# Asking for two chunks' inputs at once, moving a recurrence into the first part, and grouping attention products by kind

## Chip, cores and metric

One core of one Trainium2 chip. The metric is the device time of one launch in microseconds (us). Each kernel is run several times; nearly all times below are medians.

## The reference, cut to what matters

```python
# batch 4, heads 8, sequence 768, head dim 64
for t in range(S):
    state = gamma * state + outer(k[:, :, t], v[:, :, t])
    y[:, :, t] = scale * (q[:, :, t] @ state)
x = y.transpose(0, 2, 1, 3).reshape(3072, 512)
h = x @ w_in            # 512 -> 2048
g = maximum(0.01 * h, h)
out = g @ w_out         # 2048 -> 512
```

The inputs q, k, v are float32, the weights float64.

## The kernel before

The sequence is cut into six chunks of 128 steps. For each chunk and each of four batches (counted from 0): scores (`ap`), a masked copy of them (`am`, VectorE), then `yp` in three kinds of small products: query times state, scores times values, keys times values for the next state. VectorE writes `x` from it and updates the state `st`. The two large layers run for 512 tokens at a time with seven products M1 to M7 of a Winograd-like scheme; they need sums of weight blocks (s1, s2, s4) and differences of x (t0, t1, t2).

The float64 weights arrive in 32 pieces. ScalarE takes three steps on each (`powers`), VectorE three more (`mantissas`), during the first two chunks. In the traces here each engine runs its instructions in the order in which the Python code emits them, so that order is the schedule.

```python
def stage_y(c, b, xb):                      # one batch
    ps = two_banks(f"yp_{c}_{b}")
    if c > 0:
        for j, m, i in pairs:               # L145: 64x64 tiles
            nc.tensor.matmul(ps[...], lhsT=st[b][...], rhs=x[...])
    for j, m, i in pairs:                   # L150: 128x64 tiles
        nc.tensor.matmul(ps[...], lhsT=vs[...], rhs=am[...])
    if more:                                # L158: 128x64 tiles
        nc.tensor.matmul(sp[...], lhsT=ks[...], rhs=vs[...])
    # ... VectorE: x from ps, state from sp; then load() of the batch after next

def round_piece():                          # one weight piece
    mantissas(n)                            # VectorE
    load_piece(n + 3)                       # into one of three buffers
    powers(n + 2)                           # ScalarE, two pieces ahead
    # ... after each fourth piece: the sums of its block

# the start
load(0, 0); dec; load_piece(0); load_piece(1); load(0, 1); load_piece(2)
for b in range(B):                          # chunk 0
    scored(0, b)()
    round_piece()
    read(0, b)()
all_of(differences(*xs[0]), sums(win[0]))
# chunk 0, first block of w_in: M1, M2, M6, M5, M4, M7, M3 with, in between:
at = put(rounds(1), s0=[scored(1, 0)], s2=[read(1, 0)],
         s3=[scored(1, 1)], s5=[read(1, 1)])
# then chunk 1's batches 2 and 3, then chunk 1's first block
for b in range(2, B):
    scored(1, b)(); round_piece(); read(1, b)()
differ(1)()
```

(Cuts are marked with "..."; indices are left out.) `scored` is decay of the values on GpSimd, the score product and its masked copy; `read` is `stage_y`.

## Time and profile before

| | before |
|---|---|
| median of 3 runs | 688.67 us (688.64 to 690.79) |
| span of the profiled run | 686.5 us |
| PE busy | 663.5 us |
| M1 of the first part starts | 28.18 us |
| M6 of the second chunk starts | 64.82 us |
| first output product starts | 75.29 us |
| last product starts | 681.78 us |

The last four rows are starts of single matmuls in the trace. From the first output product on PE never waits until the last product, so the kernel splits into a head of 75.29 us, a body of 606.49 us and an end of 4.7 us. How the views are read, and their lines, stands in the prediction.

### The profile page before, as it was taken

What the parts mean: (1) busy time and instruction counts of PE and PEld (TensorE: products, weight loads), DVE (VectorE), ACT (ScalarE), POOL (GpSimd) and SP (SyncE); (2) the same over time, 40 slices, a digit from 0 to 9 for tenths busy, and PEclk for the clock granted to TensorE, in tenths of its full rate; (3) what the DMA queues carried; (4) which work ended last, traced back from release to release, by engine and by line L of the source; (5) the groups of instructions that cost most, each with busy time, mean ns of one, the idle gap of its engine ahead of it and who ended that gap; (6) DMA issues with size and microseconds to landing.
All of it is one profiled execution on the core that took longest, in us unless ns stands there. A gap on an engine that the chain in (4) does not pass through costs nothing.

```text
span 686.5 us, 9550 instructions
## 1 busy us (share of the span) xinstructions
PE 663.5 (97%) x4096; PEld 578.9 (84%) x4096; DVE 375.6 (55%) x573; ACT 166.8 (24%) x275; POOL 28.0 (4%) x29
## 2 busy tenths in 40 slices
PE   5787999999999999999999999999999999999997
PEld 5676888888888888888888888888888888888886
DVE  4878767988888765613653533553451354341342
ACT  4432455445543001311210221220221130221210
POOL 1110000000001010100100100100000000000000
PEclk9999999999999999999999999999999999999999
DMA  8741222223412453100301300301300000100001
GB/s 315 283 154 62 82 72 84 92 72 123 153 34 90 138 181 119 55 1 10 114 1 62 123 0 1 123 1 62 123 0 1 1 1 16 46 1 0 1 1 62
DMA packets 15162, 49.12 MB, mean 72 GB/s; under 512 B 1680, under 2 KB 1680, under 8 KB 15120
## 3 DMA queue, kind: packets, MB, share of 16 engines
q1 hardware_dynamic: 15120, 48.51, 20.2%
q8 instruction: 32, 0.52, 0.3%
q14 instruction: 10, 0.08, 0.0%
HBM read 42.21 MB, written 6.29 MB: 71 GB/s over the span
## 4 chain that ended last, share of the span: by engine, by line
PE 94%; DMA 3%; DVE 1%; issue 1%; POOL 0%; ACT 0%; SPq 0%; POOLq 0%
PE B_h L303 12%; PE A_o L303 12%; PE B_o L303 12%; PE C_o L303 12%; PE C_h L303 12%; PE A_h L303 12%; PE D_h L303 6%; PE D_o L303 6%; PE yp L150 3%; PE ap L126 3%; PE yp L145 1%; PE yp L158 1%; DMA qk<-in_qk_dram 1%; DMA raw<-in_weights_dram 1%; DMA kv<-in_kv_dram 1%
## 5 line engine op out<-in xcount | busy, mean ns | idle before, releaser
L303 PE MATMUL A_h<-x,win 128*128 128x256 f32 x384 | 91.0, 380 | 0.0
L303 PEld LDWEIGHTS A_h<-x,win 128*128 128x128 f32 x384 | 72.7, 190 | 10.0
L303 PE MATMUL A_o<-g,wout 128*128 128x256 f32 x288 | 68.2, 380 | 0.0
L318 ACT ACTIVATE g<-g 128x512 f32<-128x512 f32 x72 | 43.8, 630 | 86.0 <-DVE g L252 85.9
L303 PEld LDWEIGHTS A_o<-g,wout 128*128 128x128 f32 x288 | 54.6, 190 | 7.8 <-ACT g L333 0.4
L252 DVE TENSOR_TENSOR m<-m,B_h 128x512 f32<-128x512 f32 x24 | 16.5, 687 | 65.6 <-PE B_h L303 65.6
L252 DVE TENSOR_TENSOR m<-m,B_o 128x512 f32<-128x512 f32 x16 | 11.0, 686 | 66.1 <-PE B_o L303 66.1
L323 ACT COPY m<-A_h 128x512 f32<-128x512 f32 x24 | 14.1, 586 | 135.6 <-PE A_h L303 103.9
L112 POOL TENSOR_TENSOR kv<-kv,dec 128x512 f32<-128x512 f32 x24 | 27.5, 1145 | 470.3 <-DMA kv<-in_kv_dram 276.8
L303 PE MATMUL B_h<-t,win 128*128 128x256 f32 x192 | 45.5, 380 | 1.0 <-DVE t L255 1.0
L303 PE MATMUL C_h<-t,win 128*128 128x256 f32 x192 | 46.1, 383 | 0.0
L303 PE MATMUL B_h<-x,win 128*128 128x256 f32 x192 | 46.0, 382 | 0.0
L303 PE MATMUL D_h<-t,win 128*128 128x256 f32 x192 | 45.5, 380 | 0.0
L303 PE MATMUL C_h<-x,win 128*128 128x256 f32 x192 | 45.5, 380 | 0.0
L163 DVE TENSOR_TENSOR x<-yp,dec 128x512 f32<-128x512 f32 x24 | 16.6, 690 | 46.3 <-PE yp L158 33.4
L303 PEld LDWEIGHTS B_h<-t,win 128*128 128x128 f32 x192 | 36.4, 190 | 6.3 <-DVE t L255 1.4
L150 PE MATMUL yp<-am,kv 128*64 128x128 f32 x384 | 29.4, 301 | 12.1 <-issue 8.1
L303 PEld LDWEIGHTS D_h<-t,win 128*128 128x128 f32 x192 | 36.4, 190 | 5.0
L303 PEld LDWEIGHTS C_h<-x,win 128*128 128x128 f32 x192 | 36.4, 190 | 5.0
L303 PEld LDWEIGHTS C_h<-t,win 128*128 128x128 f32 x192 | 35.9, 190 | 5.4
L303 PEld LDWEIGHTS B_h<-x,win 128*128 128x128 f32 x192 | 36.0, 190 | 5.3 <-issue 0.3
L255 DVE TENSOR_TENSOR gd<-g,gd 128x512 f32<-128x512 f32 x48 | 36.8, 767 | 1.6
(88 smaller groups left out, 1006.8 us busy)
## 6 DMA issues: line engine op xcount, KB each, us to landing
raw<-in_weights_dram SPq DMA_DIRECT2D x32, 512.0 KB, 3.8
qk<-in_qk_dram SPq DMA_DIRECT2D x24, 512.0 KB, 4.8
kv<-in_kv_dram SPq DMA_DIRECT2D x24, 512.0 KB, 5.5
out_dram<-o SPq DMA_DIRECT2D x24, 256.0 KB, 2.1
dec<-decay_dram SPq DMA_DIRECT2D x1, 262.0 KB, 5.5
```

Source lines behind the costliest of these rows:

```text
L112: nc.gpsimd.tensor_tensor(out=v, in0=v, in1=gk.unsqueeze(2).to_broadcast([128, H, D]), op=ALU.mult)
L126: nc.tensor.matmul(ps[:, j, a, :], lhsT=x[ts(j, 64), 1, a, :], rhs=x[ts(j, 64), 0, a, :])
L145: nc.tensor.matmul(ps[ts(i, 64), j, m, :], lhsT=st[b][ts(j, 64), a, :], rhs=x[ts(j, 64), 0, a, :], start=(m == 0), stop=False, skip_group_ ...
L150: nc.tensor.matmul(ps[ts(i, 64), j, m, :], lhsT=vs[:, 2 * a + j, :], rhs=am[:, j, a, :], start=(c == 0 and m == 0), stop=True, skip_group_ ...
L158: nc.tensor.matmul(sp[ts(j, 64), a, :], lhsT=ks[:, 2 * a + j, :], rhs=vs[:, 2 * a + j, :], start=False, stop=True, skip_group_check=True)
L163: nc.vector.tensor_tensor(out=blocks, in0=ps[:, :, 0 : HP // 2, :], in1=gq, op=ALU.mult)
L252: nc.vector.tensor_tensor(out=out, in0=a, in1=b, op=ALU.add)
L255: nc.vector.tensor_tensor(out=out, in0=a, in1=b, op=ALU.subtract)
L303: nc.tensor.matmul(ps[:, i, :], lhsT=block(w, sa)[:, k, ts(i, 128)], rhs=rhs[:, k, :], start=(first and i == 0 and n == 0 and k == 0), sto ...
L318: nc.scalar.activation(g[:, i], g[:, i], AF.Prelu, alpha=0.01)
L323: nc.scalar.copy(out=got["m1"], in_=ps)
```

## The change

It is meant to take the waits out of the head: all inputs of the first two chunks are asked for at the start, into buffers of tiles that are used later; chunk 1's whole recurrence runs between the products of chunk 0's first block; and the products of two batches are issued kind by kind.

```diff
-    def stage_y(c, b, xb):
+    def stage_y(c, bs, xb):
+        got = [(b, *heads.pop((c, b)), scores.pop((c, b)), two_banks(...)) for b in bs]
+        for b, x, _, _, ps in got:      # query times state, all batches
+        for _, _, y, am, ps in got:     # scores times values, all batches
+        for b, _, y, _, ps in got:      # keys times values, all batches
...
     load(0, 0)
     nc.sync.dma_start(out=dec, in_=decay)
+    load(0, 1)
     load_piece(0)
     load_piece(1)
-    load(0, 1)
+    load(0, 2, new_o("in2"))
+    load(0, 3, new_o("in3"))
     load_piece(2)
+    load_piece(3, tile_x("words")...)
+    for b in range(3):
+        load(1, b, unit_tile(LATE[2 - b], f"in1{b}"))
...
     for b in range(B):
+        if b == 2:
+            next_mantissas()
+            next_powers()
         scored(0, b)()
-        round_piece()
+        if b == 2:
+            next_mantissas()
         read(0, b)()
-    all_of(differences(*xs[0]), sums(win[0]))
+    first = differences(*xs[0]), sums(0)
+    next(first[0])
+    next_mantissas()
+    next_mantissas()
+    for step in (1, 0, 1):
+        next(first[step])
...
-                at = put(rounds(1), s0=[scored(1, 0)], s2=[read(1, 0)], s3=[scored(1, 1)],
-                         s5=[read(1, 1)])
+                at = {0: [scored(1, 0)] + more, 1: [scored(1, 1)] + more,
+                      2: [read(1, 0), next_powers], 3: [read(1, 1), scored(1, 2), next_powers],
+                      4: [scored(1, 3), next_mantissas, next_powers],
+                      5: [read(1, 2), next_mantissas, next_powers], 6: [read(1, 3), differ(1)]}
             elif (c, u) == (1, 0):
-                for b in range(2, B):
-                    scored(1, b)()
-                    round_piece()
-                    read(1, b)()
-                differ(1)()
-                at = rounds(1)
+                at = rounds(1, 3)
...
-                      3: [read(2, 2 * c), read(2, 2 * c + 1)]}
+                      3: [read(2, 2 * c, 2 * c + 1)]}
...
-                          4: [read(c + 1, u), read(c + 1, u + 1)]}
+                          4: [read(c + 1, u, u + 1)]}
```

A number `k:` in `at` means: emitted after the k-th of the seven products, counted from 0, and after what that product's result needs. So `6: [read(1, 3), ...]` stands behind everything that M3 sets off.

## The prediction

> **What bounds the kernel now.** I read the page first, then busy time by stage, then the chain that ended last, then single instructions of that chain. The page's engine line and four windows:
>
> ```profile
> PE 663.5 (97%) x4096; PEld 578.9 (84%) x4096; DVE 375.6 (55%) x573; ACT 166.8 (24%) x275; POOL 28.0 (4%) x29
> ...
> 0.00:28.18 28.18, 16.56 (x192) 15.22 (x192) 14.74 (x23) 11.53 (x17) 4.67 (x9) 0.94 0.84 307
> 28.18:64.82 36.64, 29.56 (x323) 24.54 (x320) 30.42 (x48) 11.08 (x19) 4.97 (x4) 0.95 0.42 145
> 64.82:75.07 10.25, 10.25 (x47) 9.04 (x48) 7.48 (x12) 3.12 (x5) 0.00 (x0) 1.00 0.15 52
> 75.07:686.50 611.43, 607.09 (x3538) 530.13 (x3536) 322.95 (x493) 141.09 (x235) 18.33 (x16) 1.00 0.16 57
> ```
>
> Columns of a window: its length, then busy us of PE, PEld, DVE, ACT, POOL, the clock, the DMA share, GB/s. PE is idle 11.6 us until the first part's first product M1 (28.18), 7.1 us from there to 64.82, where the second chunk's product M6 starts, and then only 4.3 us, nearly all at the very end. So only the first 65 us hold idle time to win; after that a change pays only if PE itself gets less to do. In 28.18 to 64.82 DVE is busy 30.4 of 36.6 us: a nearly full second engine. The chain there:
>
> ```profile
> 46.66 4.58 DMA kv<-in_kv_dram
> ...
> 51.40 1.59 POOL kv L112
> 52.99 1.77 issue
> 54.76 1.62 PE yp L150 x16
> ...
> 60.26 0.34 DVE wout L244
> ...
> 62.05 0.60 DVE x L163
> ...
> 64.08 0.70 DVE t L255
> 64.78 0.04 issue
> 64.82 1.99 PE B_h L303 x8
> ```
>
> The values of chunk 1's batch 2 (batches count from 0) land at 51.24 us, so PE idles from 50.2 to 54.76. The "issue" before 54.76 is DVE in truth: it had the next mask product queued behind the differences of g,
>
> ```profile
> 51.99 1.53 DVE L255 TENSOR_TENSOR g<-g 128x512 f32<-128x512 f32 x1
> 53.45 1.21 DVE L129 TENSOR_TENSOR am<-ap,mask 128x1024 f32<-128x1024 f32 x1
> ```
>
> and DVE again ends the wait at 64.82. The transfers hide a VectorE chain that is almost as long.
>
> The attention products of later chunks, in the chain from 218 to 246 us (one batch, then the next):
>
> ```profile
> 229.75 0.60 PE yp L145 x16
> 230.34 1.02 PE yp L150 x16
> 231.37 0.47 PE yp L158 x16
> 231.83 0.60 PE yp L145 x16
> 232.43 1.02 PE yp L150 x16
> 233.45 0.47 PE yp L158 x16
> ```
>
> By the starts of the single matmuls, one batch takes 2.086 us: 16 of L145, 16 of L150, 16 of L158. In steady flow four of L145 start per 0.109 us, two of L150 per 0.109, two of L158 per 0.058, so 0.437 + 0.873 + 0.466 = 1.776. The other 0.31 us lies at the changes of kind: 0.05 on L145's first four, 0.11 from L145 to L150, 0.05 on L150's first two, 0.10 from L158 back to L145.
>
> **What the Trainium skill says.** (1) TensorEngine Tiling, Key Properties: changing the tiling mode drains the TensorE. The trace agrees: L145 is 64 by 64, L150 and L158 are 128 by 64, and of the gaps above all are at that change. (2) TensorE: Matmul & The Clock Gate, Part 1: after a mostly idle window of about 3.4 us the clock is halved, and a busy window frees it. The trace agrees in kind: two stretches of 3.4 us at half clock, each after an idle one:
>
> ```profile
> 21.00:24.50 3.50, 3.35 (x38) 3.26 (x40) 2.25 (x5) 1.95 (x3) 0.43 (x1) 0.51 0.75 291
> 50.40:54.70 4.30, 0.00 (x0) 0.00 (x0) 4.23 (x6) 1.32 (x3) 1.58 (x1) 1.00 0.01 3
> 54.70:58.60 3.90, 3.84 (x44) 3.75 (x46) 2.97 (x6) 0.00 (x0) 0.00 (x0) 0.56 0.43 131
> ```
>
> A window about 35% busy (17.6 to 21.0, 1.2 us of work) was enough to halve the next, one 60% busy (24.5 to 27.9) was not, and one 73% busy (10.8 to 14.2) did not free it. (3) SBUF — State Buffer, on the shared port pair of VectorE and GpSimd: an exclusive lock, also for VectorE instructions with two SBUF inputs. The trace agrees: the 1.53 us above is a 0.68 us instruction that ends 0.55 us after a decay on POOL; another (30.50) has 1.53 us too.
>
> **The change part by part.**
>
> *Inputs asked for at once.* Landings come 1.28 us apart (0.524 MB each) while the queue is full. In the new order: qk0 4.5, kv0 5.7, decay 7.2, qk1/kv1 8.5/9.8, pieces 0 and 1 11.1/12.4, batch 2 13.6/14.9, batch 3 16.2/17.5, pieces 2 and 3 18.7/20.0, chunk 1 21.3 to 30.2. Eight transfers may be under way at a time, enough for the pace. So chunk 0's batch 2 is 5 us earlier, chunk 1's last 20 us earlier: no input is waited for after 8 us.
>
> *First part up to M1.* The same until batch 1's products end at 17.5. Batch 2's scores then run at once (17.5, was 18.6), but its mask product stands on DVE behind piece 0's three conversion steps (1.86 us from first start to the next instruction): 18.49 + 1.86 = 20.35, product until 21.58, its yp at 21.67 (was 21.15). Half clock until 24.45, batch 3's mask product 25.6 to 26.8, yp 26.9, M1 at 28.42: 0.24 later than now.
>
> *M1 to the second chunk's M6.* DVE decides: x and state of batch 3 28.58, t0 29.5, pieces 2 and 3 30.1 to 33.9. M2 needs both: 34.0 (now 31.2), with PE idle from 31.4 but for piece 2's share. Then PE back to back: second scores 35.9, M6 37.0, batch 0's yp 38.9 (2.09), M5 40.9, yp 42.8, scores 44.9, M4 45.9, scores 47.9, M7 49.0, yp 50.8, M3 52.9, yp 54.7, end 56.8. The second chunk's M1 starts at 56.8 instead of 61.85. But its M6 needs t1, and on DVE batch 3's x stands behind the end of g: mask product 49.0, piece 4 50.1, three products for g 51.9 to 53.9, batch 2's x and state 53.9 to 55.3, piece 5 55.3 to 57.1, g1 57.1, ACT's Prelu 57.8 to 58.5, four differences at 0.6 to 0.73 each to 61.15, x 61.15, states 61.75 and 62.2, t0 62.5, t1 63.3 to 63.95. M6 at 64.0, against 64.82: **0.8 us won**. PE then idles from 58.7 to 64.0, 5.3 us. The idle time has moved, not gone.
>
> *Clock.* Those 5.3 us surely halve the clock for what follows, as at 54.7 now: M6 on runs some 2.6 to 6 us at half speed, mean near 4.2 by a free phase, so **2.1 us lost** after the wait. The like loss now lies before 64.82. The 2.5 us idle before M2 may do the same: 1.8 us, chance a half, **0.9 expected**; PE's delay reaches DVE through the yp products it waits for near 45 us.
>
> *After M6.* Pieces 6 and 7 and their sums (1.86 + 1.86 + 2.6 us of DVE) fit before the first output product; the transfers of pieces stay as they are. No other time moves.
>
> *Kind by kind.* A pair costs 2 x 1.776 + 0.31 = 3.86 instead of 4.17. Eight pairs (two for each of chunks 2 to 5) x 0.31 = **2.5 us won**, all of it on PE's path, where PE never waits. The x blocks and states come up to 2 us later, but before chunk 2's first M6 (259.5) DVE has about 2 us of slack, in the later chunks far more.
>
> Sum: -0.8 + 2.1 + 0.9 - 2.5 = -0.3 us. I lean a little further down, as the throttle is the least sure term: 688.67 - 0.8, so 687.9.
>
> **The rivals.** *The transfers were the whole wait.* Then the 4.6 us near 50 and its half clock go: M6 near 59, six us won and 2.5 for the pairs, 680. For it: the chain names the DMA. Against: DVE was busy 4.23 of the 4.30 us in that gap and gets one more conversion in this stretch. *VectorE takes its place and the clock falls twice*: M6 at 65.8, then 3 us lost, so +4 - 2.5: 690.2. For it: the half clock after a window 35% busy. *The grouping gives nothing*, because both batches' banks and mask products must be ready first: 690.8. Against: in all eight pairs the mask products end three products before. *No throttle at all*: 685.4.
>
> **Range and chances.** 685.2 to 690.4: from no throttle to both throttles with the pairs' gain in hand. 2% is 13.8 us, and all PE idle time before 65 us together is 18.7, of which some 11 wait on chunk 0's inputs and cold products that stay; so faster 0.01, within 2% 0.98, slower 0.01.
>
> **What would show each step.** Landings of chunk 1's keys and values before 31 us; M1 near 28.4; M2 near 34 released by DVE; the second chunk's M1 near 57 and its M6 near 64 released by t on DVE, with 5 us of PE idle between; half clock right after; pairs of yp at 3.86 us in later chunks. I am wrong if M6 comes before 62, if the clock stays full after it, or if a pair still takes 4.1 us.

## The result

The changed kernel takes 689.83 us (688.21 to 689.86, 4 runs), the kernel before 689.52 in its 4 runs: ratio 1.0006, 95% interval 0.9982 to 1.003. So the two are the same. The profiled run is the fastest of the four (the other three took 689.82 to 689.86).

Busy time of the changed kernel by stage, cut at the same four events (columns as in the prediction: length, busy us of PE, PEld, DVE, ACT, POOL, clock, DMA share, GB/s):

```profile
0.00:27.71 27.71, 15.08 (x192) 13.86 (x192) 12.15 (x17) 8.88 (x13) 6.76 (x11) 0.88 0.95 371
27.71:66.28 38.57, 30.10 (x323) 23.88 (x321) 31.67 (x50) 13.60 (x22) 2.09 (x2) 0.95 0.23 82
66.28:78.20 11.92, 11.92 (x49) 10.29 (x50) 9.24 (x16) 3.04 (x6) 0.00 (x0) 0.87 0.27 88
78.20:686.30 608.10, 604.36 (x3537) 529.59 (x3535) 321.70 (x492) 140.74 (x235) 18.97 (x16) 1.00 0.16 57
```

The first output product starts at 78.20 us instead of 75.29: the head is 2.91 us longer. The body, up to the start of the last product (682.18), takes 603.99 us instead of 606.49: 2.50 us shorter. The end differs by 0.6 us the other way. The two changes cancel.

The transfers did what they should: the last input of chunk 1 landed at 30.95 us instead of 51.24. But PE still stands still for 5.3 us, now from 61.0 to 66.28, with VectorE busy for nearly all of it, and then runs at half clock:

```profile
61.00:66.20 5.20, 0.00 (x0) 0.00 (x0) 5.03 (x10) 2.50 (x4) 0.00 (x0) 0.97 0.07 28
66.20:69.40 3.20, 3.12 (x8) 2.58 (x9) 1.27 (x2) 0.00 (x0) 0.00 (x0) 0.52 0.00 0
```

In the second window PE finishes 8 matmuls in 3.2 us. The chain that ended last, over this stretch (start, length, what):

```profile
58.69 0.69 DVE w L276
59.38 0.61 DVE g L280
...
60.01 0.64 ACT g L346
...
60.67 0.70 DVE gd L283
...
62.82 0.60 DVE g L283
63.42 0.60 DVE x L182
...
65.45 0.70 DVE t L283
...
66.28 3.44 PE B_h L331 x8
```

Batch 3's `x` (63.42) is ready to be written once its products end near 59.0, but VectorE reaches it only after a conversion, g, ScalarE's Prelu of g and the four differences of g.

The pairs of batches in later chunks, at the same place as those of the prediction:

```profile
232.62 1.03 PE yp L164 x32
233.66 1.90 PE yp L169 x32
235.56 0.93 PE yp L176 x32
```

By the starts of single matmuls such a pair takes 3.862 us, against 4.172; in the last chunk, which has no third kind, 2.932 against 3.244.

One thing of this profile was not foreseen. Two VectorE instructions between M1 and M2 took twice their usual time (timeline: start, length, engine, line, operation):

```profile
28.46 1.04 POOL L133 TENSOR_TENSOR in<-in,dec 128x512 f32<-128x512 f32 x1 [1.51 <-DMA in<-in_kv_dram]
28.76 1.28 DVE L283 TENSOR_TENSOR t<-x 128x512 f32<-128x512 f32 x1
...
31.11 1.04 POOL L133 TENSOR_TENSOR kv<-kv,dec 128x512 f32<-128x512 f32 x1 [1.61 <-DMA kv<-in_kv_dram]
31.22 1.48 DVE L276 SCALAR_TENSOR_TENSOR w<-w,z 128x512 f32<-128x512 f32 x1
```

Each ends 0.54 to 0.55 us after a decay on GpSimd (POOL) has ended: 28.46 + 1.04 + 0.54 = 30.04, and 31.11 + 1.04 + 0.55 = 32.70. Without it they take 0.68 and 0.69. The early landing itself places these decays there: each starts within 0.2 us of the landing of its values.

### The profile page after: what moved, and what is told of

The parts are those of the page before. It is cut to its first block, busy times and chain, and to the rows that moved or that the text cites. A ratio compares the mean times of both kernels' runs of the same rounds, so it can differ in the third digit from the quotient of the medians.

```text
span 686.3 us, 9531 instructions
## 1 busy us (share of the span) xinstructions
PE 661.5 (96%) x4096; PEld 577.6 (84%) x4096; DVE 374.8 (55%) x573; ACT 166.3 (24%) x275; POOL 27.8 (4%) x29
## 4 chain that ended last, share of the span: by engine, by line
PE 93%; DVE 3%; DMA 2%; issue 1%; POOL 0%; SPq 0%; ACT 0%; DVEq 0%
PE B_h L331 12%; PE A_o L331 12%; PE B_o L331 12%; PE C_o L331 12%; PE C_h L331 12%; PE A_h L331 12%; PE D_h L331 6%; PE D_o L331 6%; PE ap L147 3%; PE yp L169 3%; DMA o_in<-in_kv_dram 2%; PE yp L164 1%; PE yp L176 1%; DMA dec<-decay_dram 1%; DVE w L274 0%
## 5 line engine op out<-in xcount | busy, mean ns | idle before, releaser
L331 PE MATMUL A_h<-x,w 128*128 128x256 f32 x384 | 92.1, 383 | 3.1 <-DVE w L276 3.1
L331 PEld LDWEIGHTS A_h<-x,w 128*128 128x128 f32 x384 | 73.1, 191 | 13.7 <-issue 2.2
L331 PE MATMUL A_o<-g,w 128*128 128x256 f32 x288 | 68.2, 379 | 0.0
L331 PEld LDWEIGHTS A_o<-g,w 128*128 128x128 f32 x288 | 54.6, 190 | 7.7 <-ACT g L361 0.4
L331 PE MATMUL B_h<-t,w 128*128 128x256 f32 x192 | 47.0, 389 | 5.3 <-DVE t L283 5.3
L331 PEld LDWEIGHTS B_h<-t,w 128*128 128x128 f32 x192 | 37.4, 196 | 11.1 <-issue 5.7
L331 PE MATMUL C_h<-t,w 128*128 128x256 f32 x192 | 46.1, 383 | 0.0
L331 PE MATMUL B_h<-x,w 128*128 128x256 f32 x192 | 46.1, 383 | 0.0
L331 PE MATMUL D_h<-t,w 128*128 128x256 f32 x192 | 45.5, 380 | 0.0
L331 PE MATMUL C_h<-x,w 128*128 128x256 f32 x192 | 45.5, 380 | 0.0
```

The lines of the kernel that those rows point to most:

```text
L331: nc.tensor.matmul(ps[:, i, :], lhsT=block(w, sa)[:, k, ts(i, 128)], rhs=rhs[:, k, :], start=(first and i == 0 and n == 0 and k == 0), sto ...
```

## The experiments

Theory V: in the head VectorE's program order, and the half clock that follows a long PE wait, hold the second chunk, and not the inputs. The grouping is worth 0.31 us for each of eight pairs. Rival R: transfers set the head. Rival A: VectorE's amount of work, not its order, sets it. Twelve kernels ran, all with correct results. Events of each profiled run, in us (M1', M6' are those of the second chunk), and the ratio to the kernel before with its 95% interval:

| kernel | M1 | M1' | M6' | first output product | median | ratio |
|---|---|---|---|---|---|---|
| before | 28.18 | 61.85 | 64.82 | 75.29 | 688.1 to 689.5 | 1 |
| changed | 27.71 | 58.96 | 66.28 | 78.20 | 689.83 | 1.0006 (0.9982 to 1.003) |
| pairs_only | 27.12 | 61.41 | 64.39 | 74.85 | 685.62 | 0.9956 (0.9938 to 0.9973) |
| after_warm | 29.56 | 59.20 | 66.43 | 76.89 | 687.03 | 0.9972 (0.9949 to 0.9995) |
| x_first | 28.30 | 58.81 | 60.54 | 75.82 | 687.14 | 0.9979 (0.9961 to 0.9998) |
| recurrence_back | 29.71 | 65.04 | 68.01 | 78.47 | 688.93 | 1.0009 (0.9991 to 1.0026) |
| mask_first | 23.81 | 57.22 | 64.54 | 76.36 | 686.14 | 0.9961 (0.9938 to 0.9983) |
| x_first_b | 27.92 | 58.65 | 60.38 | 72.38 | 683.26 | 0.9930 (0.9910 to 0.9951) |
| both_first | 24.21 | 55.09 | 56.82 | 68.63 | 681.42 | 0.9896 (0.9876 to 0.9915) |
| both_warm | 25.37 | 55.21 | 56.94 | 68.88 | 679.87 | 0.9875 (0.9854 to 0.9896) |
| late_inputs | 26.48 | 56.34 | 58.07 | 70.04 | 678.71 | 0.9867 (0.9847 to 0.9887) |
| best | 23.80 | 53.80 | 55.52 | 68.01 | 680.02 | 0.9881 (0.9860 to 0.9903) |
| best_b | 23.98 | 55.47 | 57.20 | 67.56 | 677.84 | 0.9847 (0.9825 to 0.9869) |
| best_b_late | 23.01 | 54.13 | 55.86 | 66.24 | 679.33 | 0.9878 (0.9852 to 0.9904) |

(The row of before gives the range of its medians; its events are those of its one profile.) Runs of one kernel spread by some 5 us: 11 runs of before went from 685.36 to 690.18. Where the half clock falls in the head differs from run to run, so M1 of one and the same head varies (27.7 to 29.7 in the changed kernel's). This is why I read the experiments by intervals inside one trace and not by totals alone; each kernel has one trace.

### pairs_only: the grouping alone

```diff
 # the kernel before, with stage_y of the changed kernel
-    3: [read(2, 2 * c), read(2, 2 * c + 1)]
+    3: [read(2, 2 * c, 2 * c + 1)]
-    4: [read(c + 1, u), read(c + 1, u + 1)]
+    4: [read(c + 1, u, u + 1)]
```

> The kernel before with nothing but the grouping by kind in chunks 2 to 5. If the grouping is worth 0.31 us for each of eight pairs and the head of the changed kernel eats it, this one is 2.5 us faster than the kernel before (ratio about 0.9964, near 686.5 us), with its head up to 75 us unchanged and each pair of yp at 3.86 us (2.93 in the last chunk) instead of 4.17 (3.24). If the grouping only moves waits and the changed head is harmless, it is within 0.5 us of the kernel before.

The six pairs with all three kinds measure 3.862 or 3.863 us, the two of the last chunk 2.932. From the first output product to the last product the kernel takes 603.96 us, against 606.49 before: 2.53 us less, and the ratio 0.9956 (3.0 us of 688.5, interval 1.9 to 4.3) agrees. The grouping alone is the whole gain of the change; the rest of it gives that gain back.

### after_warm: PE kept busy while it waits

```diff
+            if m == warm:       # "M2" for chunk 0, "M6" for chunk 1
+                spare, (w, x, t) = bank_of("B"), tiles[0]
+                for r in range(2):
+                    ...          # M1's eight matmuls into the bank of M6,
+                    ...          # which M6 later starts afresh
```

> The changed kernel with idle PE time filled by products that nobody reads: M1 twice more into the bank of M6 ahead of M2 of the first chunk, and the same ahead of M6 of the second chunk (3.5 us of PE each, in stretches where PE waits for 3.8 and 5.3 us). If the half clock after those stretches costs what the trace suggests (1.7 us early, 1.6 us late), M6 of the second chunk comes 1 to 2 us earlier (near 64.7 instead of 66.28), runs 1.73 us instead of 3.44, and the time falls by 2 to 3 us, to about 686.5. If the half clock only covers waits that stay, the time stays within 0.5 us or rises.

The stretch that ran at half clock now runs at full clock:

```profile
61.00:66.40 5.40, 3.64 (x17) 2.85 (x16) 5.24 (x9) 2.53 (x4) 0.00 (x0) 1.00 0.10 39
66.40:69.60 3.20, 3.17 (x15) 2.81 (x16) 2.33 (x5) 0.00 (x0) 0.00 (x0) 1.00 0.00 0
```

In 3.2 us PE now finishes 15 matmuls where it finished 8. From M1 to M6' it takes 36.87 us instead of 38.57, and from M6' to the first output product 10.46 instead of 11.92: 1.70 and 1.46 us, as expected. M6' did not come earlier in absolute time, a miss, because in this run the half clock in chunk 0 lasted 10.2 us instead of 6.8 and M1 came 1.85 us later. The total (0.9972) lies below the changed kernel's 1.0006; the two intervals overlap.

### x_first: batch 3's x ahead of the end of g

```diff
-                      5: [read(1, 2), next_mantissas, next_powers], 6: [read(1, 3), differ(1)]}
+                      5: [read(1, 2), read(1, 3), differ(1)]}
             elif (c, u) == (1, 0):
-                at = rounds(1, 3)
+                at = rounds(0, 1, 3)
```

> The changed kernel with batch 3's attention products, its x and the differences of x of chunk 1 moved ahead of M3 and so ahead of g's end on VectorE, and piece 5's conversion moved behind them. If VectorE's order holds the second chunk's M6, that M6 follows its M1 with no idle time (near 60.7 instead of 66.28) at full clock; later VectorE waits may take back 1 to 3 us, so the total falls by 3 to 6 us, to 683 to 686. If the wait comes from transfers or from the amount of VectorE work alone, M6 stays within 1 us of 66 and the total within 1 us.

M6' comes at 60.54, 1.73 us after M1', with no idle time: it was VectorE's order. Amount alone (rival A) did not hold this product. But the total fell by less than expected, for a new wait. The chain that ended last:

```profile
65.93 0.70 DVE w L274
...
66.69 3.27 DMA raw<-in_weights_dram
...
71.98 0.48 ACT m L357
...
72.50 3.48 PE C_h L331 x8
```

The conversion of piece 5 is now late, so its buffer comes free late and piece 8 lands late. ScalarE's first step on piece 8 stands in program order ahead of its copy of M5, and M3' needs the bank that this copy empties. M3' ran at 72.5, at half clock.

### x_first_b: the same, with ScalarE's order mended

```diff
-                at = rounds(0, 1, 3)
+                at = {0: [next_mantissas, next_powers], 1: [next_mantissas],
+                      3: [next_mantissas, next_powers]}
...
+            if (c, u) == (0, 0):
+                put(at, s0=[next_powers])        # first output product
```

> x_first again, with ScalarE's first steps for piece 8 moved behind the copy of M5, since in x_first that copy stood behind a piece whose buffer VectorE freed late (M3 of the second chunk started at 72.5 at half clock). If that wait is what took back the gain of x_first, the second chunk's seven products run from 58.8 to about 71.5 without a long gap, and the total is 3 to 5 us below the changed kernel, 684 to 686. If the amount of VectorE work is the bound, a wait of like size shows at another product and the total stays near 687.

M1' to the first output product takes 13.72 us instead of 19.24 in the changed kernel, and the ratio is 0.9930. A wait of some 1.6 us remains: those products alone need 7 x 1.73 = 12.1.

### recurrence_back: early inputs, old place of the recurrence

```diff
-                at = {0: [scored(1, 0)] + more, 1: [scored(1, 1)] + more, ...}
+                at = {0: [scored(1, 0)] + more, 1: more,
+                      2: [read(1, 0), next_powers], 3: [scored(1, 1), next_powers],
+                      4: [next_mantissas, next_powers], 5: [read(1, 1)]}
             elif (c, u) == (1, 0):
+                for b in range(2, B):
+                    scored(1, b)(); round_piece(); read(1, b)()
+                differ(1)()
-                at = rounds(1, 3)
+                at = rounds(1)
```

> The changed kernel with chunk 1's recurrence where the kernel before had it (batches 0 and 1 inside the first part, 2 and 3 behind it), all inputs still asked for at once. If VectorE is what holds it, M6 of the second chunk comes at 66 to 68 us, as in the changed kernel or later, with a PE gap before batch 2's masked products although their inputs landed before 31 us; total 688 to 691. If transfers were the whole wait in the kernel before, that gap is gone and M6 comes near 60, the total near 682.

The gap before batch 2's masked products is there with all its inputs landed long before (chain that ended last):

```profile
53.87 0.70 DVE g L280
54.59 0.64 ACT g L346
...
57.40 0.60 DVE g L283
58.00 1.13 DVE am L150
```

The mask product of batch 2 runs at 57.9 behind the differences of g, as it did at 53.45 in the kernel before, and its `yp` at 59.24. M6' is at 68.01. Rival R is out: taking the late transfer away did not bring the second chunk forward. How little the transfer cost can be read too. From the start of M3 (51.84 here, 46.52 in the kernel before) to these products 7.40 us pass here and 8.24 in the kernel before. The difference, 0.84, is what the decay of batch 3's values, at 51.40, added to the last difference of g in the kernel before (1.53 us instead of 0.68).

### mask_first: mask products ahead of conversions in chunk 0

```diff
-        if b == 2:
-            next_mantissas()
-            next_powers()
         scored(0, b)()
+        if b >= 2:
+            next_mantissas()
         if b == 2:
-            next_mantissas()
+            next_powers()
         read(0, b)()
```

> The changed kernel with chunk 0's mask products of batches 2 and 3 ahead of the conversions of pieces 0 and 1 on VectorE, nothing else. If the conversion in front of batch 2's mask product is what keeps M1 near 28 us, M1 starts at 23 to 25 us, M2 near 30 instead of 34.6 and the second chunk's M6 near 62 instead of 66.3; the total falls by about 4 us against the changed kernel, to 684 to 686. If inputs set M1, it stays near 28 and so does the total.

M1 starts at 23.81 as expected; part of this is that no half clock is recorded before 29.8 in this run. M6' comes at 64.54, not 62, a miss. Of the 3.9 us won at M1, 2.05 are left at the six matmuls of M2 that need piece 3 (32.56 instead of 34.61; the 30 expected was for these, and only the two that need piece 2 start at 30.0). The trace shows where they went: the decays on GpSimd stay where the landings put them, and the earlier VectorE work runs into more of them. Four instructions (at 23.39, 26.19, 28.28 and 31.02) are lengthened by 0.66 to 0.88 us each; from M1 on the changed kernel has two such, at 28.76 and 31.22. The clock takes less: M2 lies in a half clock from 29.8 to 36.6, as the changed kernel's does from 35.1 to 38.6, and M6 comes 1.74 us earlier than there. M6' keeps those 1.74, behind the same wait for VectorE. The total gained 3.1 us against the changed kernel, by the difference of the two ratios times 688.5, of the 4 expected.

### both_first and both_warm: the two together, without and with filled waits

both_first is mask_first with x_first_b. both_warm adds after_warm's spare products ahead of M2 only.

> mask_first and x_first_b together. If both are waits of one chain, the gains add: the first output product near 69 to 70 us instead of 78.2, total 680 to 682. If VectorE's amount of work is the bound from there on, the first output product comes near 74 and the total near 684.

> both_first with M1 twice more into the bank of M6 while PE waits for M2 (3.5 us of PE in a stretch of 4 to 5 us of waiting). If a half clock follows that wait in both_first, this is 1 to 1.7 us faster; if none does, equal within 0.5 us.

The gains add: the first output product comes at 68.63. The ratios are 0.9896 and 0.9875; their intervals overlap. From M1 to M6' the warm one takes 31.57 us instead of 32.61, and its four runs lie within 0.7 us (679.54 to 680.20), where the six of both_first spread over 2.8. So the spare products earn about 1 us in these two traces, in which both_first has a half clock at 30.6 to 34.0 and both_warm none. That they take away the scatter is not shown: late_inputs, best and best_b_late have them too, and their six runs spread over 3.2 to 5.1 us.

### late_inputs: transfers as before, in the better order

```diff
-    load(0, 2, new_o("in2")); load(0, 3, new_o("in3"))
     load_piece(2)
-    load_piece(3, ...)
-    for b in range(3):
-        load(1, b, ...)
-        if b == 0:
-            load(1, 3)
-            if c > 1 and n < NC * B:
+            if n < NC * B and n - 2 * B not in range(AHEAD):
-        if n != 3:
-            load_piece(n + 4 if n < 3 else n + 3)
+        load_piece(n + 3)
```

> both_warm with the transfers asked for as in the kernel before: batches two at a time, pieces three at a time, each when its buffer comes free. If asking for everything at once is what the better VectorE order needs, chunk 1's batches 2 and 3 (needed near 43 and 46 us) come late and the total rises by 2 to 4 us over both_warm, to 682 to 684. If the transfers are hidden either way, it stays within 1 us of both_warm, near 680.

The ratio is 0.9867 against 0.9875: nothing lost. I had expected either outcome to be possible, and it is the second: asking for everything at once earns nothing here either, although the last batch's keys and values now land at 48.74 us. (Its profile is of the slowest of its six runs.)

### best and best_b: conversions moved into VectorE's idle time

```diff
-                at = {0: [scored(1, 0)] + more, 1: [scored(1, 1)] + more,
-                      2: [read(1, 0), next_powers], 3: [read(1, 1), scored(1, 2), next_powers],
+                at = {0: [scored(1, 0)] + more, 1: [scored(1, 1), next_powers] + more,
+                      2: [read(1, 0), next_mantissas, next_powers],
+                      3: [read(1, 1), scored(1, 2), next_powers],
                       4: [scored(1, 3), next_mantissas, next_powers],
                       5: [read(1, 2), read(1, 3), differ(1)]}
             elif (c, u) == (1, 0):
-                at = {0: [next_mantissas, next_powers], 1: [next_mantissas],
-                      3: [next_mantissas, next_powers]}
+                at = rounds(1, 3)                                  # best
+                at = {1: [round_piece], 3: [next_mantissas]}       # best_b
                # best leaves out x_first_b's put(at, s0=[next_powers]); best_b has it
```

> both_warm with the conversions of pieces 4 and 5 moved into VectorE's idle time near 40 and 47 us, so that after the second chunk's M6 only pieces 6 and 7 are left. If VectorE's backlog there is the last wait (about 1.6 us of PE idle between 64 and 71 us in both_warm), the total falls by 1 to 2 us to 678 to 679; if something else holds PE there, it stays within 0.5 us of both_warm.

> best with ScalarE's first steps of piece 9 moved behind the first output product: in best they stood ahead of the Prelu of M2 and waited for piece 9, whose buffer comes free only with piece 6's conversion, so PE waited 2 us before the first output product (68.0) and half a clock followed. If that wait is what ate the gain of best, the first output product comes near 66, without a half clock behind it, and the total is 676.5 to 678. If VectorE's backlog holds PE anyway, the wait moves to the second output product and the total stays near 679.5.

In best the seven products of the second chunk ran without a gap from 53.80, but the first output product waited 2 us, until 68.01, for ScalarE, which stood at piece 9 as x_first's had at piece 8; its total, 680.02 us, is no gain over both_warm. best_b moves that step: 677.84 us, ratio 0.9847, the lowest (its interval overlaps those of late_inputs and both_warm), with no half clock in the records of its head, which begin at 12.4 us. From M6' to the first output product it takes 10.36 us, six products back to back. What is left there is 0.3 us ahead of the second output product.

### best_b_late: best_b with the transfers as before

> best_b with the transfers asked for as in the kernel before. If late asking costs nothing once VectorE's order is right, it is within 1 us of best_b; if the tighter order needs chunk 1's batches 2 and 3 earlier (they land near 44.5 and 48.7 us when asked late), it is 1 to 3 us slower.

The ratio is 0.9878 with an interval that overlaps that of best_b, so the totals do not decide. The profile shows a wait that best_b lacks (chain that ended last):

```profile
39.99 4.99 DMA qk<-in_qk_dram
...
45.11 1.18 PE ap L147 x16
```

PE is idle for 1.5 us, from 43.59 to 45.11, until batch 3's queries have landed. So only in the tightest order does a late transfer show in the chain, at under 2 us, and in this very run the first output product was still earlier (66.24, with M1 1 us earlier). Whether asking early is worth 1 us or nothing there stays open.

## Why the prediction was right, point by point

The forecast of "same" held, 687.9 against 689.83 measured, inside its range. Its parts, with the profile's numbers:

- **The first reading** was wrong in one place. The values that land at 51.24 us are not batch 2's. The first two chunks have eight decays, one for each batch in order, and these are the seventh and the eighth (timeline of the kernel before):

```profile
44.08 1.04 POOL L112 TENSOR_TENSOR kv<-kv,dec 128x512 f32<-128x512 f32 x1 [8.04 <-DMA kv<-in_kv_dram]
51.40 1.58 POOL L112 TENSOR_TENSOR kv<-kv,dec 128x512 f32<-128x512 f32 x1 [6.28 <-DMA kv<-in_kv_dram]
```

  So batch 2's values were there by 44.08, and 51.24 is batch 3's landing, which batch 2's products do not need. The chain names it only because its decay was the last event on GpSimd before them. The wait until 54.76 was VectorE's from the start. The transfers did not hide a VectorE chain; in this wait they cost 0.85 us, by the one blocked instruction. The forecast survives this, because it let VectorE decide, but the wait that the early inputs were to take away was hardly there.
- **Kind by kind**: 3.86 us for a pair and 2.5 us in all were predicted; 3.862 and 2.50 were measured. This step was exact, since it summed gaps read from single matmuls.
- **Inputs**: landings until 30.2 us were predicted, 30.95 measured. That no input is waited for afterwards held, and so did that this alone brings nothing (recurrence_back). The trace bears out the eight transfers at a time: the changed kernel never has more than eight between issue and landing, and from the ninth (4.95 us) to 23.34 us each is issued just after a landing.
- **M1**: 28.42 predicted, 27.71 measured, close partly by luck. Batch 1's products ended at 15.1 us instead of 17.5, with the clock full from 11.25 on, where the records begin; then a half clock of 6.8 us (18.08 to 24.90) took most of that back, where the kernel before has one of 3.4 to 24.45, which the prediction kept. Batch 2's mask product did stand behind piece 0's conversion (18.70 us); mask_first, which moves only that order, brought M1 to 23.81.
- **M1 to M6'**: without a half clock 35.6 us were predicted, 38.57 measured. The missing 3.0 us: 1.3 between M1 and the part of M2 that needs piece 3 (34.61) from the two VectorE instructions blocked by GpSimd, 1.2 from the half clock at 35.1 to 38.6 on M2 (which I had put in at 0.9, as an even chance of 1.8), and 0.5 over all the rest. The blocked instructions are the one term that the sum lacked. I had cited the lock and counted it as a cost of the kernel before; I did not ask where the decays of chunk 1 would fall once their inputs landed early.
- **M6' released by t on VectorE**, with 5.3 us of PE idle before it: predicted and measured (5.3, from 61.0 to 66.28). x_first shows that the order of VectorE causes it.
- **Half clock after that wait**: 2.1 us predicted, 1.45 measured (11.92 against 10.47 us to the first output product); after_warm shows that it is the clock.
- **Sum**: for the head +2.2 was predicted (-0.8 + 0.9 + 2.1), +2.91 measured; for the body -2.5 and -2.50. The net is +0.4 up to the last product where I had said -0.3, and I leaned a further 0.5 down. That lean had no number behind it and was wrong. The "0.8 us won" at M6' was wrong in sign: M6' came 1.46 us later than in the kernel before.

Of the rivals, "the transfers were the whole wait" fell with recurrence_back, and "the grouping gives nothing" with pairs_only. "No throttle at all" fell with the half clocks recorded at 35.1 and 65.9 us. "VectorE takes its place and the clock falls twice", with M6' at 65.8, is nearest to what the profile of the changed kernel shows (66.28), except that VectorE had held that place before.

## What to carry to other kernels

When a wait for a transfer is to be removed, first find out which buffer that transfer fills, and whether the waiting instruction reads it. Then list what each in-order engine does in that stretch: if another engine is busy for nearly all of it, the wait will only change its name, and the order on that engine is the thing to mend. Look at what an earlier arrival sets off elsewhere (here decays on GpSimd that block VectorE, and a ScalarE step that waits for a buffer ahead of a copy that PE needs). Small products of different tile shapes are best grouped by shape, and a PE wait of some 3 us that can't be removed may be worth filling.

## What the Trainium skill lacked or had wrong

- TensorEngine Tiling, Key Properties, says that a change of tiling mode drains the array but gives no cost. Here it is 0.31 us for one round from 64 by 64 tiles to 128 by 64 and back, and grouping two batches saved exactly one round (4.172 to 3.862 us).
- TensorE: Matmul & The Clock Gate, Part 1, gives windows of about 3.4 us that are idle or busy, without saying how busy ("mostly idle" is the prediction's wording). The clock records of the 14 traces here, cut into windows of 3.41 us and set beside PE's busy share by the profile, agree with two thresholds. At full clock, all 17 windows at most 42% busy were followed by half clock, none of those at least 52% busy was, and of the five between 43% and 49% one was. At half clock, all 8 windows at most 78% busy were followed by another, and all 18 of at least 82% by full clock. Spare products for 3.5 of 5.4 idle us were enough to keep it (after_warm).
- DMA: Bandwidth & Descriptors, Specifications, lists 358 GB/s as the limit of HBM for one core. The changed kernel, a program on one core, moved 407 GB/s between 18.08 and 24.9 us, and landings of 0.524 MB came 1.28 us apart, which is 410. So the row is no ceiling for such a program (single-core measurements further down that page exceed it too).
- No page that I read says that the clock records may begin late: the first is at 17.6 us in the profile before (11.1 to 18.2 in the 14 profiles), and earlier windows of that profile print a clock of 1.00 although single score products took 0.418 us there instead of 0.272.
